# Seven half-width block products in place of eight for two of four batches in a fused mLSTM and gated-cosine kernel

## The chip, the cores and the metric

The kernel runs on one core of a Trainium2 chip. The metric is the device time of one execution in microseconds (us). Beside the times there is one profiled execution. In its listings PE is TensorE with its matmuls, PEld the weight loads of TensorE, DVE is VectorE, ACT is ScalarE, POOL is GpSimd, and SP is the engine whose queue issues most DMA transfers (SPq).

## What is computed

An mLSTM cell with 8 heads of 40 runs over 4 batches of 768 steps. Its output, 3072 rows of 320, goes through a layer with a gated cosine. All data are float32. The scan over time is cut here to its last lines.

```python
def _attn_ref(q, k, v, i_gate, f_gate, o_gate):
    B, H, S, D = q.shape            # 4, 8, 768, 40
    for t in range(S):
        ...
        o = 1.0 / (1.0 + np.exp(-o_gate[:, :, t]))
        y[:, :, t] = o * h_tilde / denom

def _moe_ref(x, w_in, w_out):       # x: 3072 x 320, w_in: 320 x 2048, w_out: 2048 x 320
    h = x @ w_in
    g = h * np.cos(h)
    return g @ w_out
```

The change concerns the last product, g @ w_out, alone.

## The kernel before, in words

The time axis is cut into NC = 6 chunks of C = 128 steps. A chunk c of batch b is cell n = 4c + b. The layer for chunk c needs the cells of that chunk of all four batches, so the layer works one chunk behind: `both_parts(c, b)` computes cell (c+1)*4 + b and a quarter of the layer for chunk c. `first_cells` does the four cells of chunk 0 ahead of the loop. In chunk 5 of the layer no cell is left.

The layer. The 2048 inner columns are 16 blocks of 128, taken two at a time: f2 runs from 0 to 7, and `both_parts` handles f2 = 2b in its first half and 2b + 1 in its second. `Up(c, f2)` multiplies (L613, L616) into two PSUM banks `pup`, one for each of the two blocks e, with the 512 columns being 128 steps of each of four batches. ACT rounds (`near`, L621), DVE takes the remainder (`rest`, L624), ACT takes the sine (`sin`, L629), and DVE multiplies (`gate`, L633) into a tile `g` of 128 x 512, kept as `gs[c, f]`. `down(c, f2)` (L645) then multiplies, for each of the two blocks and each batch, the 128 x 128 part of `g` (the stationary operand, loaded as weights) with the 128 x 320 rows of `w_out_sb`, and accumulates over all 16 blocks in one PSUM tile `po[c][b]` for each batch. So a call is 8 matmuls of 320 columns. On the last call of a chunk (f2 = 7) the matmuls are ordered by batch, and each batch is copied by ACT to `o_sb` (L648, two buffers) and sent out by SP (L649).

Order. The whole order is written out by hand (`tc.manual_schedule()`), and each engine runs its instructions in that order. `down` is called half an iteration after its gates: in the first half of `both_parts`, `down(c, f2 - 1)`, or for b = 0 the last call of the chunk before, `down(c - 1, 7)`; in the second half `down(c, f2)`. On ACT, the first half stands in this order: `near` twice, `sin` twice, then `decay` (L379), the exponential of the next cell's matrix E, and then whatever `down` gives to ACT. The exponential waits for the mask on POOL (`decay_exponents`, L371), and the mask for a subtraction on DVE (L370). After `down`, PE goes on with the cell's values (`values_turned`, L482 and L488), then `Up(c, f2 + 1)`, then the state update (`seam`, L580). DVE's normalisation of the cell (`normalize_turned`, L502 to L514) comes after them, followed by `fade` (L565) and the second half's `rest`.

POOL also scales the keys for the state (`weigh_k`, L392) and, in chunk 0 alone, finishes the weights: the weights come in as float64 bits and are turned into float32 by `parts` (ACT) and `join` (DVE, with the last addition on POOL, L149).

Pools. PSUM has two banks for `ps_a` (the cell), two for `ps_u` (`pup`) and four for `ps_o` (`po`). A wait between engines is set for each tile; a PSUM tile here is a bank or a part of one.

Of the kernel before, what the change touches and what calls it, by code (L numbers as in the profile page):

```python
# [11 lines left out]
FP = mybir.dt.float32  # L12
# [4 lines left out]
OP = mybir.AluOpType  # L17
# [12 lines left out]
def kernel(  # L30
# [20 lines left out]
    nc = tc.nc  # L51

    B, H, S, D = q.shape
    C = 128
    NC = S // C
# [3 lines left out]
    DM = H * D  # L59
    DFF = moe_w_in.shape[1]  # L60
    NF = DFF // 128
# [13 lines left out]
    p2 = ctx.enter_context(tc.tile_pool(name="p2", bufs=2))  # L75
    p3 = ctx.enter_context(tc.tile_pool(name="p3", bufs=3))
    p4 = ctx.enter_context(tc.tile_pool(name="p4", bufs=4))
    pb = ctx.enter_context(tc.tile_pool(name="pb", bufs=5))
    pc = ctx.enter_context(tc.tile_pool(name="pc", bufs=3))
# [3 lines left out]
    ps_o = ctx.enter_context(tc.tile_pool(name="ps_o", bufs=4, space=bass.MemoryType.PSUM))  # L83
# [15 lines left out]
    p1 = ctx.enter_context(tc.tile_pool(name="p1", bufs=1))  # L99
# [20 lines left out]
    w_out_sb = wp.tile([128, NF, DM], FP, name="w_out_sb")  # L120
# [11 lines left out]
    def parts(dst, bits):  # L132
        n = dst.shape[1]
        hi, lo = bits[:, 0:n, 1], bits[:, 0:n, 0].bitcast(U32)
        t = p2.tile([128, WQ], I32, name="wt", tag="wt")[:, 0:n]
        m = p2.tile([128, WQ], I32, name="wm", tag="wm")[:, 0:n]

        nc.scalar.activation(out=t.bitcast(FP), in_=hi.bitcast(FP), func=AF.Abs)

        nc.scalar.activation(out=m, in_=lo, func=AF.Copy, scale=2.0 ** -29)  # L140
        return dst, hi, t, m
# [164 lines left out]
    def sigmoid(c, bs=slice(0, B)):  # L306
        o = sig[c][:, bs.start * DM:bs.stop * DM]
        nc.scalar.activation(out=o, in_=o, func=AF.Sigmoid)
# [51 lines left out]
    def psum_o():  # L360
        return ps_o.tile([128, HP, C], FP, name="pm", tag="o")

    def cols(n, j, width):
        c, b = divmod(n, B)
        return tab[:, c, j, ts(b, H)].unsqueeze(2).to_broadcast([128, H, width])


    def decay_exponents(n):
        E = Es[n]
        nc.vector.tensor_tensor(out=E, in0=E, in1=cols(n, 0, C), op=OP.subtract)  # L370
        nc.gpsimd.affine_select(out=E, in_=E, compare_op=OP.is_ge, fill=1.0e30, base=0,  # L371
                                pattern=[[0, H], [1, C]], channel_multiplier=-1)
# [5 lines left out]
    def decay(n):  # L378
        nc.scalar.activation(out=Es[n], in_=Es[n], func=AF.Exp, scale=-1.0)  # L379
# [9 lines left out]
    def weigh_k(n):  # L389
        if n < N - B:  # L390
            kw = p2.tile([128, H, D], FP, name="kw", tag="kw")
            nc.gpsimd.tensor_tensor(out=kw, in0=ks[n % NB][:, :, 0:D], in1=cols(n, 1, D), op=OP.mult)  # L392
            kws[n] = kw
# [44 lines left out]
    def scores(n):  # L438
        pool, tag = psum(n)
        qT, kT = qkT[n]  # L440
        ps = [pool.tile([128, HP, C], FP, name="ps", tag=tag) for _ in range(2)]
        for p in range(HP):
            for j in range(2):
                r = slice(64 * j, 64 * j + (64 if n < TURNED else D))
                nc.tensor.matmul(ps[j][:, p], kT[r, p], qT[r, p], start=True, stop=True)  # L445
        pss[n] = ps

    def weigh(n):
        for j in range(2):
            w = Es[n].rearrange("p (a j) t -> p a j t", j=2)[:, :, j]  # L450
            nc.vector.tensor_tensor(out=w, in0=pss[n][j], in1=w, op=OP.mult)  # L451

    def values_kept(n):

        pool, tag = (ps_o, "o") if n == B else psum(n)
        heads_of[n] = None
        if n >= B:
            pq = pool.tile([128, H, D1], FP, name="pq", tag=tag)
            for p in range(HP):
                nc.tensor.matmul(pq[:, 2 * p:2 * p + 2].rearrange("p j d -> p (j d)"), qkT[n][0][:, p],  # L460
                                 st[n % B][:, p].rearrange("p j d -> p (j d)"), start=True, stop=True)
            heads_of[n] = pq
# [136 lines left out]
    gs, po = {}, {}  # L599

    class Up:
# [29 lines left out]
        def gate(self, e):  # L631
# [2 lines left out]
                                           op0=OP.mult, op1=OP.mult)  # L634
            gs[self.c, 2 * self.f2 + e] = g

    def down(c, f2):
        if f2 == 0:
            po[c] = [ps_o.tile([128, DM], FP, name="po", tag="o") for _ in range(B)]

        order = [(f, b) for f in (2 * f2, 2 * f2 + 1) for b in range(B)]
        if f2 == NF // 2 - 1:
            order.sort(key=lambda fb: fb[1])
        for f, b in order:
            nc.tensor.matmul(po[c][b], gs[c, f][:, ts(b, C)], w_out_sb[:, f], start=(f == 0), stop=(f == NF - 1))  # L645
            if f == NF - 1:
                o = p2.tile([128, DM], FP, name="o_sb", tag="o_sb")
                nc.scalar.copy(out=o, in_=po[c][b])  # L648
                nc.sync.dma_start(out=out[b * S + c * C:b * S + (c + 1) * C], in_=o)  # L649


    pw, pmu = (ps_u.tile([128, HP, C], FP, name=name, tag="up") for name in ("pw", "pmu"))
# [1 line left out]
    def warm(k, bank=None):  # L654

        for _ in range(k):
            nc.tensor.matmul(bank or pw, nil, nil.unsqueeze(1).to_broadcast([128, HP, 128]), start=True, stop=True)  # L657
# [122 lines left out]
    def out_parts():  # L780
        p, piece = outs.pop(0)
        return p, parts(*piece)

    def out_join(p, h, last=None):
        join(*h, last)
        if p + 3 < NF // 2:
            outs.append((p + 3, weights_out(p + 3)))

    def both_parts(c, b):

        n = (c + 1) * B + b
        cell = n < N
        begin = c == b == 0
        more = cell and n + 1 < N
        f2 = 2 * b
        up = Up(c, f2)
        if cell:  # L800
            scores(n)
            if begin:
                values_kept(n)

                warm(6, psum_o())
        for e in range(2):
            up.near(e)
        if begin:
            weigh(n)
        for e in range(2):  # L810
            up.rest(e)
        if cell and not begin:
            weigh(n)
        if begin or more and c > 0:
            decay_exponents(n + 1)
        for e in range(2):
            up.sin(e)
            up.gate(e)
        if c == 0 and b == 1:
            sigmoid(1, slice(1, B))  # L820
        if b == B - 1 and c + 2 < NC:
            sigmoid(c + 2)
        h = ()
        if begin:
            h = out_parts()
            w = parts(*pieces.pop(0))
        else:
            if c == 0:
                out_join(*out_parts())
            if pieces:  # L830
                join(*parts(*pieces.pop(0)))
        if begin or more and c > 0:
            decay(n + 1)
        elif more:
            decay_by_bias(n + 1)
        if f2 > 0:
            down(c, f2 - 1)
        elif c > 0:
            down(c - 1, NF // 2 - 1)
        if cell:  # L840
            if n + 2 < N:
                load(n + 2)
            if n < TURNED:
                if not begin:
                    values_kept(n)
                values(n)
                normalize(n)
            else:
                values_turned(n)
            if begin:  # L850
                out_join(*h, nc.vector)
            if TURNED <= n + 2 < N:
                load_G(n + 2)
            if n + 3 < N:
                load_E(n + 3)
            if b == B - 2 and c + 2 < NC:
                load_o(c + 2)
            if n >= TURNED:
                normalize_turned(n)
            fade(n)  # L860
        h = w if begin else ()
        if not begin:
            sin_next()
        if pieces and not begin:
            h = parts(*pieces.pop(0))
        up = Up(c, f2 + 1)
        if cell:
            seam(n)
        for e in range(2):
            up.near(e)  # L870
        for e in range(2):
            up.rest(e)
        if cell and n < TURNED:
            seam_out(n)
        if h:
            join(*h)
        if cell:
            state(n)
        for e in range(2):
            up.sin(e)  # L880
            up.gate(e)
        if more:
            weigh_k(n + 1)
        if pieces:
            join(*parts(*pieces.pop(0)))
        down(c, f2)
        if pieces:
            join(*parts(*pieces.pop(0)))
        if c == 0:
            if b + 2 < B:  # L890
                pieces.extend(weights_in(b + 2))
            h = out_parts()
        if more and n + 1 < TURNED:
            turn(n + 1)
            turn_out(n + 1, c > 0)
        elif more:
            turn_blocks(n + 1)
        if c == 0:
            out_join(*h)
# [38 lines left out]
```

## Time and profile before

| | us |
|---|---|
| median of 4 runs | 551.47 |
| range of the runs | 550.1 to 551.79 |
| the profiled execution's own time | 550.1 |
| its span, first to last instruction | 548.4 |

The profiled execution's mean granted TensorE clock was 0.997. The groups that bear on the change, from the list of groups by line (us busy in total, mean ns of one):

| line, engine, what | count | busy us | mean ns |
|---|---|---|---|
| L645 PE, down | 768 | 219.3 | 439 |
| L613 PE, up | 384 | 175.0 | 598 |
| L645 PEld, its weight loads | 768 | 142.0 | 190 |
| L371 POOL, mask of E | 19 | 20.7 | 1091 |
| L392 POOL, keys scaled | 20 | 14.4 | 722 |
| L648 ACT, output copied from PSUM | 24 | | 425 (median) |
| L649 SPq, output issued | 24 | | 349 (median) |

How to read it: durations of matmuls and loads overlap those of their neighbours, so the busy time of a group is less than count times mean, and what a matmul costs in a stream is seen from the distance of starts. A timeline line gives start, length, engine, line, operation, tiles and, in brackets, idle time before it and what ended it. The float32 matmul is carried out as two passes, each with its weight load, so counts are twice those of the program.

### The profile page before, as it was taken

To read this page: it belongs to the slowest core of one execution; us is meant where nothing else is said; L and a number is where in the kernel's file an instruction comes from. 1 tells how busy PE (TensorE), PEld (TensorE's weight loads), DVE (VectorE), ACT (ScalarE), POOL (GpSimd) and SP (SyncE) were. 2 spreads that over 40 slices of the span, in tenths; PEclk is the share of its full clock that TensorE was granted. 3 is DMA by queue.
4 is the path that set the end of the run, shared out by engine and by line. 5 is a ranking of instruction groups with operands and counts; after the bars stand their busy time and mean duration, and the time that the engine had idled before them with its cause. 6 is when DMAs were issued, how large, how long until landed. Compare 5 with 4: busy or idle time off the path is not lost.

```text
span 548.4 us, 9153 instructions
## 1 busy us (share of the span) xinstructions
PE 538.0 (98%) x3395; PEld 316.7 (58%) x3395; DVE 355.7 (65%) x692; ACT 264.4 (48%) x420; POOL 76.5 (14%) x112
## 2 busy tenths in 40 slices
PE   9989899999999999999999999999999999999997
PEld 6865566665565565565565555555555655555554
DVE  5877987967767677677677667667666666232311
ACT  4868796775632543633445344427335423231312
POOL 5531433523110110100101101100000000000000
PEclk9989999999999999999999999999999999999999
DMA  9999995961366761166735076635075000100001
GB/s 146 208 229 222 236 226 136 194 125 28 87 138 126 148 129 30 58 131 135 152 83 99 26 158 135 141 79 117 3 175 110 7 14 12 53 0 1 0 0 49
DMA packets 134509, 56.82 MB, mean 104 GB/s; under 512 B 72081, under 2 KB 130529, under 8 KB 134465
## 3 DMA queue, kind: packets, MB, share of 16 engines
q1 hardware_dynamic: 134320, 56.04, 47.3%
q8 instruction: 27, 0.44, 0.4%
q0 software_dynamic: 96, 0.18, 0.2%
q14 instruction: 18, 0.14, 0.1%
q10 hardware_dynamic: 48, 0.02, 0.0%
HBM read 50.00 MB, written 6.21 MB: 103 GB/s over the span
## 4 chain that ended last, share of the span: by engine, by line
PE 89%; DVE 4%; DMA 3%; ACT 1%; issue 1%; SPq 0%; POOL 0%; ACTq 0%; DVEq 0%; POOLq 0%
PE po L645 37%; PE pup L613 29%; PE pup L616 9%; PE ps L445 4%; PE hp L488 3%; PE hp L482 2%; PE ph L470 2%; PE pu L580 1%; PE pw L657 1%; DMA o<-in_o_gate_dram 1%; DMA ks<-in_k_dram 1%; PE pt L426 1%; DMA bits<-in_moe_w_out_dram 1%; PE px L573 1%; DVE wt L148 1%
## 5 line engine op out<-in xcount | busy, mean ns | idle before, releaser
L645 PE MATMUL po<-w_out_sb,g 128*128 128x320 f32 x768 | 219.3, 439 | 1.3 <-POOL w_out_sb L149 1.0
L645 PEld LDWEIGHTS po<-w_out_sb,g 128*128 128x128 f32 x768 | 142.0, 190 | 67.0 <-issue 8.3
L613 PE MATMUL pup<-xT,w_in_sb 128*128 128x512 f32 x384 | 175.0, 598 | 1.1 <-POOL w_in_sb L149 0.6
L621 ACT ACTIVATE n<-pup 128x512 int32<-128x512 f32 x96 | 52.0, 593 | 213.2 <-PE pup L616 213.2
L624 DVE SCALAR_TENSOR_TENSOR n<-pup,n 128x512 f32<-128x512 f32 x96 | 61.8, 686 | 135.1 <-ACT n L621 135.1
L613 PEld LDWEIGHTS pup<-xT,w_in_sb 128*128 128x128 f32 x384 | 70.9, 190 | 77.5 <-issue 64.2
L629 ACT ACTIVATE n<-n 128x512 f32<-128x512 f32 x96 | 58.8, 630 | 11.9 <-DVE n L624 11.9
L633 DVE SCALAR_TENSOR_TENSOR g<-pup,n 128x512 f32<-128x512 f32 x96 | 61.7, 684 | 1.7
L371 POOL TENSOR_SCALAR_AFFINE_SELECT E<-E 128x1024 f32<-128x1024 f32 x19 | 20.7, 1091 | 291.1 <-DVE E L370 268.1
L616 PE MATMUL pup<-xT,w_in_l 64*128 64x512 f32 x192 | 54.2, 641 | 0.0
L616 PEld LDWEIGHTS pup<-xT,w_in_l 64*128 64x128 f32 x192 | 14.4, 184 | 36.4 <-issue 35.6
L451 DVE TENSOR_TENSOR E<-ps,E 128x512 f32<-128x512 f32 x48 | 30.7, 680 | 4.7 <-PE ps L445 4.7
L379 ACT ACTIVATE E<-E 128x1024 f32<-128x1024 f32 x21 | 22.2, 1057 | 22.3 <-POOL E L371 16.3
L410 DVE STREAM_TRANSPOSE t<-qs 128x512 f32<-128x512 f32 x32 | 32.3, 1086 | 0.0
L445 PEld LDWEIGHTS ps<-t,t 40*128 40x128 f32 (+1 forms) x384 | 25.1, 188 | 9.7 <-issue 9.2
L445 PE MATMUL ps<-t,t 40*128 40x128 f32 (+1 forms) x384 | 25.8, 274 | 0.0
L379 ACT ACT_TABLE_LOAD x18 | 23.1, 1283 | 0.3
L778 ACT ACT_TABLE_LOAD x18 | 23.1, 1283 | 0.3
L502 DVE STREAM_TRANSPOSE room<-hp 128x128 f32<-128x128 f32 x32 | 8.6, 306 | 22.5 <-PE hp L488 22.5
L370 DVE TENSOR_TENSOR E<-E,tab 128x1024 f32<-128x1024 f32 x19 | 23.1, 1215 | 0.0
L488 PE MATMUL hp<-E,vs 128*32 128x128 f32 x512 | 17.3, 276 | 0.0
L417 DVE STREAM_TRANSPOSE room<-o 128x256 f32<-128x256 f32 x32 | 17.2, 617 | 0.0
(128 smaller groups left out, 427.9 us busy)
## 6 DMA issues: line engine op xcount, KB each, us to landing
E<-M_d SPq DMA_DIRECT2D x22, 512.0 KB
bits<-in_moe_w_in_dram SPq DMA_DIRECT2D x40, 128.0 KB
bits<-in_moe_w_out_dram SPq DMA_DIRECT2D x8, 640.0 KB
room<-G_d SPq DMA_DIRECT2D x32, 128.0 KB
ks<-in_k_dram SPq DMA_DIRECT2D x24, 160.0 KB
vs<-in_v_dram SPq DMA_DIRECT2D x24, 160.0 KB
out_dram<-o_sb SPq DMA_DIRECT2D x24, 160.0 KB
qs<-in_q_dram SPq DMA_DIRECT2D x32, 80.0 KB
```

The lines of the kernel that those rows point to most:

```text
L379: nc.scalar.activation(out=Es[n], in_=Es[n], func=AF.Exp, scale=-1.0)
L410: nc.vector.transpose(out=dst.rearrange("r p (t x) -> r p x t", x=T4), in_=src.rearrange("r p (x d) -> r p x d", x=T4)[:, :, :, 0:32])
L445: nc.tensor.matmul(ps[j][:, p], kT[r, p], qT[r, p], start=True, stop=True)
L451: nc.vector.tensor_tensor(out=w, in0=pss[n][j], in1=w, op=OP.mult)
L488: nc.tensor.matmul(hps[n][j][ts(p, 32), half], vs[n % NB][:, h, lo:lo + DA], Es[n][:, h], start=False, stop=True, skip_group_check=True)
L613: nc.tensor.matmul(pu, w_in_sb[:, i, ts(block(f2, e), 128)], x(i), start=(i == 0), stop=False)
L616: nc.tensor.matmul(pu, w_in_l[r, f2], x(NK, r), start=False, stop=True)
L621: nc.scalar.activation(out=self.n[e], in_=self.pu[e], func=AF.Copy, bias=0.25)
L624: nc.vector.scalar_tensor_tensor(out=self.n[e].bitcast(FP), in0=self.pu[e], scalar=0.25, in1=self.n[e], op0=OP.add, op1=OP.subtract)
L629: nc.scalar.activation(out=r, in_=r, func=AF.Sin, scale=TWO_PI_DOWN)
L633: nc.vector.scalar_tensor_tensor(out=g, in0=self.pu[e], scalar=TWO_PI, in1=self.n[e].bitcast(FP), op0=OP.mult, op1=OP.mult)
L645: nc.tensor.matmul(po[c][b], gs[c, f][:, ts(b, C)], w_out_sb[:, f], start=(f == 0), stop=(f == NF - 1))
```

## The change

For chunks 1 to 5 (`parted(c)`), the products of batches 0 and 1 with a pair of blocks are formed as a 2 x 2 block product with seven multiplications in place of eight (the scheme of Strassen in Winograd's form). The left factor has four 128 x 128 parts: batch 0 or 1, block 0 or 1. The right factor has four 128 x 160 parts: block 0 or 1, left or right half of the columns. Batches 2 and 3 are multiplied as before (`whole`).

- `differences` (POOL): four 128 x 160 combinations of the w_out parts for each pair p, once, kept in `T`; done two pairs at a time (`two_differences`), at the end of chunk 0 and in chunk 1.
- `sums` (POOL): four 128 x 128 combinations of the g parts for each call, in `sg`, placed after the gates.
- `down_parted` (PE): 4 matmuls of 320 columns, then 7 of 160 columns. The seven products accumulate over all eight pairs: six stand in banks 0 and 1, three each; the seventh region, `Ps[6]`, stands in bank 2 beside batch 2's 320 columns.
- At the last pair of a chunk, batches 2 and 3 are copied by ACT and sent as before. `Ps[0]` is copied by ACT, and seven additions on DVE combine the products into the outputs of batches 0 and 1, which are then sent. In the very last call of the program the seven products come first, and batches 3 and 2 after them.

```diff
+    def differences(p, T):
+        B11, B12, B21, B22 = (w_out_sb[:, 2 * p + e, ts(h, DH)] for e in range(2) for h in range(2))
+        for i, (x, y) in enumerate(((B12, B11), (B22, T[:, 0]), (B22, B12), (T[:, 1], B21))):
+            nc.gpsimd.tensor_tensor(out=T[:, i], in0=x, in1=y, op=OP.subtract)
+        Ts[p] = T
...
+    def sums(c, f2):
...
+        S = p2.tile([128, 4, C], FP, name="sg", tag="wt")
+        A11, A21, A12, A22 = (gs[c, 2 * f2 + e][:, ts(b, C)] for e in range(2) for b in range(2))
+        for i, (x, y, op) in enumerate(((A21, A22, OP.add), (S[:, 0], A11, OP.subtract),
+                                        (A11, A21, OP.subtract), (A12, S[:, 1], OP.subtract))):
+            nc.gpsimd.tensor_tensor(out=S[:, i], in0=x, in1=y, op=op)
...
+    def down_parted(c, f2):
+        end = f2 == NF // 2 - 1
...
+            po[c] = [ps_o.tile([128, 3 * DH + 32], FP, name="po", tag="o") for _ in range(4)]
+        banks = po[c]
+        Ps = [banks[i // 3][:, ts(i % 3, DH)] for i in range(6)] + [banks[2][:, DM:DM + DH]]
...
+        def whole(bs=range(2, B)):
+            for b in bs:
+                for e, (g, w) in enumerate(((g0, w0), (g1, w1))):
+                    product(banks[b][:, 0:DM], g[:, ts(b, C)], w, e == 0)
+                if end:
+                    o = p2.tile([128, DM], FP, name="o_sb", tag="o_sb")
+                    nc.scalar.copy(out=o, in_=banks[b][:, 0:DM])
+                    result(c, b, o)
+        very_end = end and c == NC - 1
+        if not very_end:
+            whole()
+        product(Ps[0], g0[:, 0:C], w0[:, lo], True)
+        product(Ps[1], g1[:, 0:C], w1[:, lo], False)
+        product(Ps[3], g1[:, C:2 * C], T[:, 3], True)
+        product(Ps[4], S[:, 0], T[:, 0], False)
+        product(Ps[5], S[:, 1], T[:, 1], False)
+        product(Ps[6], S[:, 2], T[:, 2], False)
+        product(Ps[2], S[:, 3], w1[:, hi], False)
+        if end:
...
+            nc.scalar.copy(out=U[:, 0], in_=Ps[0])
+            for dst, x, y, op in ((o0[:, lo], U[:, 0], Ps[1], OP.add), (U[:, 0], U[:, 0], Ps[5], OP.add),
+                                  (U[:, 1], U[:, 0], Ps[6], OP.add), (U[:, 0], U[:, 0], Ps[4], OP.add),
+                                  (o0[:, hi], U[:, 0], Ps[2], OP.add), (o1[:, lo], U[:, 1], Ps[3], OP.subtract),
+                                  (o1[:, hi], U[:, 1], Ps[4], OP.add)):
+                nc.vector.tensor_tensor(out=dst, in0=x, in1=y, op=op)
+            if very_end:
+                whole((3, 2))
+            for b, o in enumerate((o0, o1)):
+                result(c, b, o)
...
     def down(c, f2):
+        if parted(c):
+            down_parted(c, f2)
+            return
...
         for e in range(2):
             up.sin(e)
             up.gate(e)
+        sums(c, f2)
...
         for e in range(2):
             up.sin(e)
             up.gate(e)
+        sums(c, f2 + 1)
         if more:
             weigh_k(n + 1)
+        if c == 0 and b == B - 1 or c == 1 and b < B - 1:
+            two_differences(c * (2 * b + 2))
```

More of the change, by code (lines that the diff above doesn't have):

```diff
@@ L635, in gate, with parted, two_differences @@
             gs[self.c, 2 * self.f2 + e] = g
+    DH = DM // 2
+    Ts, sg = {}, {}
+    def parted(c):
+        return c > 0
+    def differences(p, T):
[3 more added lines that the diff above has]
+        Ts[p] = T
+    def two_differences(p):
+        if p < 6:
+            T = pc.tile([128, 2, 4, DH], FP, name="T", tag="bits")
+            for e in range(2):
+                differences(p + e, T[:, e])
+        else:
+            for e in range(2):
+                differences(p + e, pb.tile([128, 4, DH], FP, name="T", tag="bits"))
@@ new lines, in sums @@
+    def sums(c, f2):
+        if not parted(c):
+            return
[4 more added lines that the diff above has]
+            nc.gpsimd.tensor_tensor(out=S[:, i], in0=x, in1=y, op=op)
+        sg[c, f2] = S
@@ new lines, in down_parted, with product @@
+    def down_parted(c, f2):
+        end = f2 == NF // 2 - 1
+        if f2 == 0:
+            po[c] = [ps_o.tile([128, 3 * DH + 32], FP, name="po", tag="o") for _ in range(4)]
+        banks = po[c]
+        Ps = [banks[i // 3][:, ts(i % 3, DH)] for i in range(6)] + [banks[2][:, DM:DM + DH]]
+        g0, g1 = (gs[c, 2 * f2 + e] for e in range(2))
+        w0, w1 = (w_out_sb[:, 2 * f2 + e] for e in range(2))
+        S, T = sg[c, f2], Ts[f2]
+        lo, hi = slice(0, DH), slice(DH, DM)
+        def product(out, g, w, first):
+            nc.tensor.matmul(out, g, w, start=(f2 == 0 and first), stop=end, skip_group_check=True)
+        def whole(bs=range(2, B)):
[17 more added lines that the diff above has]
+        if end:
+            o2 = p2.tile([128, 2, DM], FP, name="o2", tag="wm")
+            o0, o1 = (o2[:, b] for b in range(2))
+            U = p1.tile([128, 2, DH], FP, name="hs", tag="hs")
+            nc.scalar.copy(out=U[:, 0], in_=Ps[0])
[8 more added lines that the diff above has]
+                result(c, b, o)
@@ L637, in down, with result @@
+    def result(c, b, o):
+        nc.sync.dma_start(out=out[b * S + c * C:b * S + (c + 1) * C], in_=o)
     def down(c, f2):
+        if parted(c):
+            down_parted(c, f2)
+            return
         if f2 == 0:
@@ L648, in down @@
                 nc.scalar.copy(out=o, in_=po[c][b])
-                nc.sync.dma_start(out=out[b * S + c * C:b * S + (c + 1) * C], in_=o)
+                result(c, b, o)
     pw, pmu = (ps_u.tile([128, HP, C], FP, name=name, tag="up") for name in ("pw", "pmu"))
```

## The prediction

> **What bounds the kernel now.** I read the page's busy shares first, then the chain of work that ended last.
>
> ```profile
> PE 538.0 (98%) x3395; PEld 316.7 (58%) x3395; DVE 355.7 (65%) x692; ACT 264.4 (48%) x420; POOL 76.5 (14%) x112
> ...
> PE 89%; DVE 4%; DMA 3%; ACT 1%; issue 1%; SPq 0%; POOL 0%; ACTq 0%; DVEq 0%; POOLq 0%
> ```
>
> TensorE (PE) is busy nearly throughout, and 89% of the chain is matmuls. So each ns that a matmul pass saves shortens the kernel, each ns that PE idles lengthens it, and work on POOL or DVE is free until PE waits for it. The list of groups by shape shows what a pass is:
>
> ```profile
> L645 PE MATMUL po<-w_out_sb,g 128*128 128x320 f32 x768 | 219.3, 439 | 1.3 <-POOL w_out_sb L149 1.0 <-DVE w_out_sb L149 0.3
> ...
> L470 PE MATMUL ph<-vs,E 128*128 128x41 f32 x128 | 15.5, 282 | 0.2 <-DVE E L451 0.2
> ```
>
> A float32 matmul is two passes: 6 chunks x 16 blocks x 4 batches is 384, and the row has 768. A pass's own duration (439 ns) holds its latency; what counts is the distance from one start to the next. The timeline of the weight loads gives it:
>
> ```profile
> 8.93 0.97 PEld L357 LDWEIGHTS pm<-M_rows,ident 128*128 128x128 f32 x8
> ...
> 30.78 1.86 PEld L470 LDWEIGHTS ph<-vs,E 128*128 128x128 f32 x16
> ...
> 301.44 0.19 PEld L613 LDWEIGHTS pup<-xT,w_in_sb 128*128 128x128 f32 x1 [0.24 <-issue]
> 301.87 0.19 PEld L613 LDWEIGHTS pup<-xT,w_in_sb 128*128 128x128 f32 x1 [0.24 <-issue]
> ```
>
> 512 columns: 0.43 us apart, 0.84 ns a column. 41 columns would stream in 0.034, yet sixteen loads take 1.86: (1.86-0.19)/15 = 0.111. 128 columns: (0.97-0.19)/7 = 0.111. So a pass costs the larger of 0.111 (its weight load) and 0.84 ns a column.
>
> **The sum on PE.** The change acts on chunks 1 to 5, 8 pairs each: 40 calls. A call was 16 passes of 320 columns, 0.269 each: 4.30 us. (The timeline's 16 loads last 4.07 = 0.11 for the first, exposed load + 14 x 0.269 + 0.19.) Now 8 such passes stay (2.15), and 7 products x 2 passes have 160 columns: 0.134 by the column, and I take 0.136 for a small fixed part: 1.90. Gain 0.248 a call, x 40 = **9.9 us**. Only beyond 2.15/14 = 0.154 would there be none.
>
> A rule speaks against this: the Trainium skill, "TensorE: Matmul & The Clock Gate", section "The mechanism", says that a weight load overlaps a running matmul only when the row groups differ. Here every load fills all 128 rows. By that rule a narrow pass would be 0.107+0.134 = 0.241, so 14 of them 3.37, a loss of 1.2 us a call, 49 in all. But by it the 320-column pass would be 0.376, and it is 0.269; L357's 0.111 also excludes it. The rows decide.
>
> **What is hidden.** POOL gets four 128x128 sums a call, after the second gate. Nearest row: 128x320 (L392) 722 ns; so about 0.4 each, 1.7 a call, some 65 us in all, on an engine 86% idle. They are needed half an iteration later (gates end 310.77, the next down begins at 317.30): slack over 5 us. The exponentials' mask (L371) stands ahead of them; weigh_k behind them is wanted only in the next iteration. The weight differences, 32 of 128x160 at about 0.45, come in four bursts of 3.6 us behind weigh_k; in chunk 0 that is from 127.2 to 131, before the last w_out join (135.44). A DVE operation with two SBUF inputs may wait for a POOL one: the z product beside L386 took 1.17 us against 0.39 mean, but the gates read PSUM and took 681 ns either way. They finish about 1 us or more before PE wants their banks. Cost 0; without this cover, up to 1.7 a call. The added waits of PE on POOL, if already satisfied, cost nothing: loads with such waits also start 0.111 apart.
>
> **Where the cover is missing.** At a chunk's last pair, PE finishes batch 2 in bank 2, ACT copies it out, and the sixth product goes into the same bank. In the built program's order, exactly these products carry a wait on ACT besides POOL. That copy stands on ACT behind the exponential of the next cell. The timeline of such an end (chunk 2's):
>
> ```profile
> 306.06 4.58 PE L645 MATMUL po<-w_out_sb,g 128*128 128x320 f32 x16
> ...
> 308.36 1.21 DVE L370 TENSOR_TENSOR E<-E,tab 128x1024 f32<-128x1024 f32 x1
> ...
> 309.71 1.09 POOL L371 TENSOR_SCALAR_AFFINE_SELECT E<-E 128x1024 f32<-128x1024 f32 x1 [19.34 <-DVE E L370]
> ...
> 310.83 1.06 ACT L379 ACTIVATE E<-E 128x1024 f32<-128x1024 f32 x1 [1.62 <-POOL E L371]
> ...
> 311.80 0.73 ACT L648 COPY o_sb<-po 128x320 f32<-128x320 f32 x2
> ```
>
> Mask, exponential and copy come one after the other, and the first copy (425 ns) ends at 312.2. Before, PE had no need of it. Now the sixth product is due at 306.06 + 0.10 + 8x0.269 + 10x0.136 = 309.67. It must wait until 312.2, plus 0.06 to wake and 0.107 for a load with no matmul over it: **2.7 us**. Behind it in PE's queue stand the seventh product, the cell's values and the next Up: all is late. The ends of chunks 1 and 3 have the same distances (down 221.55, copy 227.29; 390.57 and 396.31): 3 x 2.7 = **8.1 us**. Bounds: 0 if the wait is for something earlier, 8.5 as computed with slower waking. Chunk 4 ends beside no cell: copy from about 475.2 to 475.6, product due at 476.06: free.
>
> **The clock.** 2.7 us without a matmul may cost more. Windows of 3.4 us on the clock's own grid, with their granted clock (the number before the DMA share):
>
> ```profile
> 30.50:33.90 3.40, 2.89 (x36) 2.51 (x33) 3.01 (x5) 3.11 (x10) 1.27 (x1) 1.00 1.15 121
> 33.90:37.30 3.40, 2.79 (x11) 1.78 (x10) 3.23 (x10) 0.41 (x2) 1.26 (x1) 0.50 1.00 253
> 37.30:40.70 3.40, 3.18 (x24) 1.64 (x23) 1.69 (x3) 2.48 (x6) 1.50 (x2) 1.00 1.11 345
> ```
>
> The same skill page, section "What's actually happening", has the clock fall to half after a whole idle window of about 3.4 us; by it 2.7 us costs nothing. But the window at 30.5 had no gap over 0.6 us, and the next ran at half clock. It held mostly 41-column passes; from columns x 0.84 ns its array streamed 39% of the time. Windows at 53% and more (95 us, for one) kept the clock. A window that holds most of the 2.7 us streams 20 to 40%. With the limit between 39 and 53%, it must hold 1.6 to 2.0 us of the stall, which a random phase does in 6 to 9 of 10. Each half window loses 1.7 us of matmuls. I take two of three: **3.4 us** (0 to 5.1).
>
> **Chunk ends on DVE, and the tail.** Seven additions of 128x160 (L596, 40x164 with PSUM, has 318 ns: about 0.32 each, chained) and a short copy are 2.6 us after the seventh product, at four places inside. They delay the turned normalisation; by the timeline it is done at 315.8 and DVE's next work came at 318.1. With the stall both move: DVE would be ready near 319.4, as PE's Up ends (319.2) and its first result reaches DVE at 319.9; the hp banks are free by 318, PE wants them at 319.2. Just covered. Four PSUM copies fall to two, which also ends ACT's wait for output transfers (2.76 us, off the path). At the very end batch 2's matmuls share bank 2 with the sixth product and wait for the third addition: about 1.5 after the seventh product against 1.08 of batch 3, so 0.5 with its load. Then SP issues batch 2 and behind it batches 0 and 1 (median 349 ns each): 0.7 more, and three 160 KB transfers close together, up to 0.8. Tail **+1.5 us** (1.0 to 2.3).
>
> **Sum** against the profiled run (span 548.4, own time 550.1): -9.9 + 8.1 + 3.4 + 1.5 = +3.1, so 553.2. The four runs' median is 551.47, 1.4 above that run; the forecast for a median is **554.6 us**. About 0.2% (1.1 us) is what a measurement of this kernel can tell from no change.
>
> **The rivals.**
> - No clock loss: the stalls stand, the page's rule holds or the phases miss. -0.3: 551.2, no change. For it: the rule. Against it: the 39% window. Chance 0.2, with the case of a single half window.
> - No stall: the sixth product doesn't wait for the copy, or ACT gets to it earlier. -9.9+1.5: about **543**, faster. For it: every other part of the change is covered. Against it: the order on ACT and the wait on that product. It decides when the copy ends before 309.7. Chance 0.14.
> - Exposed loads: narrow passes above 0.154, up to 0.241, 600 us. L357 and L470 exclude it; 0.02.
> - The forecast, the stalls with two or three half windows: 0.64, its own range 552.6 to 557.
>
> The range is 550.4 to 557.5: it takes in the first rival and leaves out the second and third. Chances: faster 0.15, same 0.2, slower 0.65.
>
> **What would show it.** The row of 160-column passes x560 with starts 0.136 apart (0.154 would break the gain). In the waits, PE for the output copy, 3 times, about 2.6 us each; if absent, the second rival. Slices with a granted clock of 7 or 8 tenths near 225, 309 and 393; if absent, the first. POOL's busy time near 155 us, with no wait of PE on it.

## The result and the profile after

| | before | after |
|---|---|---|
| median us | 551.26 (55 runs) | 552.81 (34 runs) |
| lowest to highest | 549.04 to 552.13 | 549.35 to 558.72 |
| ratio, 95% interval | | 1.0035 [1.0023, 1.0048] |
| profiled execution: own time, span | 550.1, 548.4 | 554.27, 552.4 |
| its mean granted TensorE clock | 0.997 | 0.986 |

By the ratio of the means the kernel became 0.35% slower, by 1.9 us; the medians differ by 1.55. Two of the runs after, at 558.1 and 558.7 us, count as slow and are left out of the ratio. The forecast was 3.1 us slower, 0.56%. First the page of the kernel after: busy shares, the clock row and the chain that ended last.

```profile
PE 532.3 (96%) x3635; PEld 337.0 (61%) x3635; DVE 369.0 (67%) x727; ACT 261.7 (47%) x415; POOL 168.0 (30%) x304
...
PEclk9799999999999999899999899999999999999999
...
PE 82%; DVE 9%; ACT 3%; POOL 2%; issue 1%; SPq 1%; DMA 1%; POOLq 0%; DVEq 0%; ACTq 0%
```

PE is busy for 96% of a longer span, where it was 98%: it has begun to wait. (Its share of the chain, 82% for 89%, is no proof of that: it is 82% and 83% in the two cures below too, where PE is busy for 98%.) The clock row has an 8 in slices 17 and 23, at about 225 and 310 us, where it had only nines before; the 7 in slice 2 belongs to the first cells. In the new kernel's lines L689 is a matmul of `down_parted`, L672 a sum on POOL, L697 the copy of a whole batch, L714 the small copy of `Ps[0]` and L719 the additions. For the wait, the list of groups by shape:

```profile
L689 PE MATMUL po<-w_out_sb,g 128*128 128x320 f32 x320 | 97.0, 445 | 0.4 <-DVE hs L719 0.4
...
L689 PE MATMUL po<-T,sg 128*128 128x160 f32 x240 | 40.0, 301 | 7.5 <-POOL sg L672 7.5
```

Nearly all new idle time of PE in the layer, 7.5 us, stands before products with a sum from POOL (0.4 more is in the tail). The row names POOL as what ended it. The timeline of the end of chunk 2 shows that this name is wrong:

```profile
302.32 0.46 POOL L672 TENSOR_TENSOR sg<-g 128x128 f32<-128x128 f32 x1 [7.99 <-DVE g L633]
...
303.69 0.46 POOL L672 TENSOR_TENSOR sg<-g,sg 128x128 f32<-128x128 f32 x1
...
311.34 0.71 PE L689 MATMUL po<-T,sg 128*128 128x160 f32 x4
...
313.04 1.06 ACT L379 ACTIVATE E<-E 128x1024 f32<-128x1024 f32 x1 [1.62 <-POOL E L371]
...
314.00 0.73 ACT L697 COPY o_sb<-po 128x320 f32<-128x320 f32 x2
...
314.55 0.66 PE L689 MATMUL po<-T,sg 128*128 128x160 f32 x2 [2.51 <-POOL sg L672]
```

The sums for this pair were done at 304.15, seven microseconds before PE came to them. (POOL was by then at the next chunk's sums, and one of those ended near 314.5.) What ended just before PE went on is the first of the two ACT copies, 314.00 + 0.41; it stands behind the exponential. In all three stalls the load of the waiting product starts 0.11 us after that copy's end. A sum of the next chunk ends within 0.01 us of it in all three as well, for the exponential and these sums both follow the mask; the second experiment below tells the two apart. The product waited for both engines, and the profile put the wait down to the wrong one.

The clock, in windows along the clock's own grid (PEclk is the granted clock), at chunk 1's end and at this one. A window at half clock is called a half window below.

```profile
core 0: us, PE busy (x) PEld busy (x) DVE busy (x) ACT busy (x) POOL busy (x), PEclk, DMA share, GB/s
...
226.00:229.40 3.40, 1.73 (x52) 1.39 (x56) 0.64 (x3) 2.59 (x5) 1.85 (x5) 1.00 0.27 95
229.40:232.80 3.40, 3.40 (x28) 1.83 (x20) 3.16 (x14) 0.88 (x2) 0.00 (x0) 0.51 0.32 103
...
311.40:314.80 3.40, 0.89 (x7) 0.68 (x6) 1.58 (x3) 1.71 (x4) 2.69 (x5) 1.00 0.00 0
314.80:318.20 3.40, 3.40 (x65) 2.57 (x67) 1.96 (x7) 1.78 (x3) 0.13 (x1) 0.50 0.27 96
```

After each of these stalls PE is busy for a whole window, at half its clock.

The sum of the two profiled executions, by stretches of the timeline from the first Up matmul of one chunk to that of the next; the clock column is half the length of the half-clock windows in the stretch that delay matmuls:

| stretch | before | after | difference | of it clock | new calls | stall |
|---|---|---|---|---|---|---|
| first cells | 38.14 | 39.71 | +1.57 | +1.71 | 0 | |
| layer chunk 0 | 93.40 | 93.40 | 0 | 0 | 0 | |
| chunk 1 | 84.53 | 82.79 | -1.74 | 0 | 7 | |
| chunk 2 | 84.51 | 86.89 | +2.38 | +1.71 | 8 | yes |
| chunk 3 | 84.51 | 86.79 | +2.28 | +1.71 | 8 | yes |
| chunk 4 | 82.77 | 83.50 | +0.73 | 0 | 8 | yes |
| chunk 5 and end | 80.49 | 79.32 | -1.17 | 0 | 9 | |

A chunk's last call falls into the next stretch, so chunk 1 has seven new calls and no stall: -1.74 / 7 = -0.25 a call. The calls themselves say the same: from a call's first matmul to the Up matmul behind it 4.159 us, where it was 4.411, so 0.252 less. Chunk 4 has a stall without a lost window: +0.73 + 8 x 0.252 = 2.7. The first cells are untouched by the change. All the kernels here share them, and their profiles have one or two half windows there; in this pair it was two after and one before.

### The profile page after: what moved, and what is told of

The parts are those of the page before. It is cut to its first block, busy times and chain, and to the rows that moved or that the text cites. A ratio compares the mean times of both kernels' runs of the same rounds, so it can differ in the third digit from the quotient of the medians.

```text
span 552.4 us, 9941 instructions
## 1 busy us (share of the span) xinstructions
PE 532.3 (96%) x3635; PEld 337.0 (61%) x3635; DVE 369.0 (67%) x727; ACT 261.7 (47%) x415; POOL 168.0 (30%) x304
## 4 chain that ended last, share of the span: by engine, by line
PE 82%; DVE 9%; ACT 3%; POOL 2%; issue 1%; SPq 1%; DMA 1%; POOLq 0%; DVEq 0%; ACTq 0%
PE po L689 29%; PE pup L613 29%; PE pup L616 9%; PE po L739 4%; PE hp L488 3%; PE ps L445 3%; PE hp L482 2%; DVE n L624 1%; PE pu L580 1%; DVE wt L146 1%; PE ph L470 1%; DVE wt L148 1%; DVE E L370 1%; DMA o<-in_o_gate_dram 1%; DVE E L451 1%
## 5 line engine op out<-in xcount | busy, mean ns | idle before, releaser
L689 PE MATMUL po<-w_out_sb,g 128*128 128x320 f32 (+1 forms) x480 | 118.9, 397 | 0.4 <-DVE hs L719 0.4
L689 PEld LDWEIGHTS po<-w_out_sb,g 128*128 128x128 f32 x480 | 83.5, 190 | 37.4 <-issue 9.1
L672 POOL TENSOR_TENSOR sg<-g 128x128 f32<-128x128 f32 x80 | 36.5, 457 | 204.2 <-DVE g L633 202.7
L689 PE MATMUL po<-T,sg 128*128 128x160 f32 x240 | 40.0, 301 | 7.5 <-POOL sg L672 7.5
L689 PEld LDWEIGHTS po<-T,sg 128*128 128x128 f32 x240 | 34.8, 190 | 8.2 <-POOL sg L672 8.2
L739 PE MATMUL po<-w_out_sb,g 128*128 128x320 f32 x128 | 36.6, 439 | 1.3 <-POOL w_out_sb L149 1.0
L739 PEld LDWEIGHTS po<-w_out_sb,g 128*128 128x128 f32 x128 | 23.7, 190 | 11.0 <-POOL w_out_sb L149 1.3
```

Source lines behind the costliest of these rows:

```text
L672: nc.gpsimd.tensor_tensor(out=S[:, i], in0=x, in1=y, op=op)
L689: nc.tensor.matmul(out, g, w, start=(f2 == 0 and first), stop=end, skip_group_check=True)
```

## The experiments

My theory was that of the prediction: three stalls on the late copy, and half-clock windows as their consequence. The rivals: the sums on POOL (which the profile itself names), and a clock that falls because the passes are narrow.

**The sixth product ahead of batch 2.** At the ends of chunks 1 to 4 the product that shares bank 2 is issued before batch 2, so no copy comes between.

```diff
+        if end and not very_end:
+            product(Ps[6], S[:, 2], T[:, 2], False)
         if not very_end:
             whole()
...
-        product(Ps[6], S[:, 2], T[:, 2], False)
+        if not end or very_end:
+            product(Ps[6], S[:, 2], T[:, 2], False)
```

> At the ends of chunks 1 to 4 the sixth product is issued before batch 2, so it no longer shares its bank with a copy that is still to come. My theory (three stalls of 2.67 us on the copy of batch 2, each able to cost a clock window): the waits go, the granted clock returns to that of before, and the time is before - 40 x 0.254 + 1.1 of tail = about 542.3 us, ratio 0.984. Rival A (the wait is for the sums on POOL, as the list of waits names it): unchanged, near 552.8. Rival B (the half windows come from the narrow passes, not from the stalls): the stalls go but the clock stays near 0.989, about 545.

Measured: 542.52 us, ratio 0.9846 [0.9833, 0.986]. The stall is gone: stretches 2 and 3 took 82.84 and 82.85 where 86.89 and 86.79 had been. No half window is left after the first cells, and the profiled clock is 0.993. Both rivals fall: the sums on POOL are unchanged and nobody waits for them, and the narrow passes are all there. One small wait was new:

```profile
226.71 0.31 ACT L717 COPY hs<-po 128x160 f32<-128x160 f32 x1
227.05 0.32 DVE L722 TENSOR_TENSOR o<-hs,po 128x160 f32<-128x160 f32 x1 [1.99 <-ACT hs L717]
...
230.72 0.71 DVE L511 TENSOR_TENSOR room<-room,hp 128x256 f32<-128x256 f32 x2
...
231.24 0.51 PE L580 MATMUL pu<-vs,kw 128*40 128x41 f32 x16 [0.27 <-DVE room L511]
```

The small copy still stands behind the exponential, so the seven additions and with them the normalisation come late, and PE's seam waits 0.3 us for its bank. With the stall gone this is the next in line.

**The copies ahead of the exponential.** The bank stays shared; ACT does the copies first.

```diff
+        late = b == 0 and c > 1
-        if begin or more and c > 0:
+        if begin or more and c > 0 and not late:
             decay(n + 1)
-        elif more:
+        elif more and not late:
             decay_by_bias(n + 1)
...
             down(c - 1, NF // 2 - 1)
+        if late and more:
+            decay(n + 1)
```

> The sixth product and the copy stay in one bank, but at the first cell of chunks 2 to 5 ACT does the copies before the next cell's exponential. Theory (the copy is late only because it stands behind the exponential, 312.2 where 309.7 was needed): the copy ends near 308.4, no stall, 542 to 543, as in the first experiment; the exponential moves by about 0.3 us and nobody waits for it. If the shared bank itself or the sums were the cause: unchanged, 552.8.

Measured: 541.21 us, ratio 0.9823 [0.9809, 0.9836], the fastest of all. Its timeline at the end of chunk 2:

```profile
302.69 2.96 PE L689 MATMUL po<-w_out_sb,g 128*128 128x320 f32 x12
...
304.44 0.41 ACT L697 COPY o_sb<-po 128x320 f32<-128x320 f32 x1
...
305.76 0.98 PE L689 MATMUL po<-T,sg 128*128 128x160 f32 x6
...
307.04 0.29 ACT L714 COPY hs<-po 128x160 f32<-128x160 f32 x1 [1.48 <-PE po L689]
307.36 1.28 ACT L379 ACT_TABLE_LOAD   x1
...
308.65 1.06 ACT L379 ACTIVATE E<-E 128x1024 f32<-128x1024 f32 x1
```

The copy is done at 304.85, before the sixth product is due, and the six passes, the sixth product's among them, run without a break. The next chunk's sums on POOL, one of which ended just as PE went on in the stalls, begin only at 307.54 here, after these passes, so PE doesn't wait for those either. The small copy is early too, so the seam waits for nobody: stretches 2 and 3 take 82.50, which is 84.51 - 8 x 0.252 = 82.49. The exponential ends 7.02 us after the down began (309.71 against 302.69), 1.2 us later than the 5.83 of before (311.89 against 306.06), not the 0.3 that I had put down: its table load (1.28 us) now stands behind the copies too. Nobody waited for it.

**The stalls filled.** Before the sixth product PE runs matmuls of zeros into a free bank, as long as the stall lasts or for a part of it. Nothing reads that bank's zeros.

```diff
+        if end and c < NC - 2:
+            warm(11, ps_a.tile([128, HP, C], FP, name="fill", tag="a"))
         product(Ps[6], S[:, 2], T[:, 2], False)
```

> The stalls stay, but PE runs eleven bf16 matmuls of zeros (0.215 us each, 2.4 us) in each of the three, before the sixth product. Theory (idle time in a window halves the next one): the time between instructions stays as it is, the half windows at 229 and 315 us are gone, and the median falls by the 3.4 us that I charged to the clock, to about 549.5, with a spread as narrow as before. Rival (the skill page's whole idle window is needed, and the half windows have another cause): unchanged, 552.8 with its wide spread.

> As the run with eleven matmuls of zeros, but five (1.1 us): each stall keeps its length, and 1.4 us of it stay idle. Theory (a window of 3.4 us must hold 1.6 to 2.0 us of idle time to halve the next): no half window after 100 us, the same time as with eleven, about 549.8. Rival (any gap of over a microsecond counts): half windows in some runs, time between 549.8 and 552.8.

> Two matmuls of zeros: 2.1 us of each stall stay idle, in one piece, at the limit that I estimated. Theory: a phase must put nearly the whole gap in one window, which 4 to 6 of 10 do, so half windows come back, fewer than without the filling: median 551 to 552.5, spread of several us. Rival (a gap must be nearly a whole window of 3.4 us, or the half windows had another cause): as with eleven, 549.8.

| matmuls of zeros | idle in a stall, about | median us | lowest to highest | ratio to before | median of the runs' granted clock |
|---|---|---|---|---|---|
| 0 (the change as it is) | 2.5 | 552.81 | 549.35 to 558.72 | 1.0035 | 0.989 |
| 2 | 2.1 | 550.99 | 548.54 to 552.06 | 0.9994 | 0.992 |
| 5 | 1.4 | 548.48 | 548.05 to 550.91 | 0.997 | 0.998 |
| 11 | 0.1 | 549.76 | 547.82 to 551.08 | 0.9987 | 0.995 |

The profile with eleven, at the end of chunk 1:

```profile
223.53 2.54 PE L753 MATMUL fill<-nil 128*128 128x512 bf16 x11
...
225.65 0.73 ACT L697 COPY o_sb<-po 128x320 f32<-128x320 f32 x2
226.20 0.51 PE L689 MATMUL po<-T,sg 128*128 128x160 f32 x2
```

The sixth product still waits for the copy, so each stall costs its 2.7 us as before (stretches 2 and 3 take 85.25 against 82.50 without a stall), and yet the median is 3.1 us lower, or 2.6 by the ratios to the runs of the kernel before that stand beside each: that part was the clock, and it was the idle time that brought it. With five the profile has no half window in the layer either. Five lies below eleven, but their ratios to before, 0.997 [0.9955, 0.9985] and 0.9987 [0.9973, 1.0], overlap; runs also differ by one or two half windows of 1.7 us in the first cells, which these kernels share with the one before. With two, the result lies just below what I had put down (551 to 552.5). Its one profile has no half window at the stalls, but its runs' clocks (0.986 to 0.999) are on the whole lower than with five (0.990 to 0.999), so some probably had them. The ratios' intervals with two, [0.9979, 1.001], and with five overlap slightly, so this step is not shown. How many of its windows belong to the stalls and how many to the first cells, the clocks of the runs don't tell.

**POOL's sums twice.** On top of the first experiment.

```diff
         sg[c, f2] = S
+        R2 = p1.tile([128, 2, C], FP, name="sg2", tag="sg2")
+        for i, (x, y, op) in enumerate(((A21, A22, OP.add), (R2[:, 0], A11, OP.subtract),
+                                        (A11, A21, OP.subtract), (A12, R2[:, 1], OP.subtract))):
+            nc.gpsimd.tensor_tensor(out=R2[:, i % 2], in0=x, in1=y, op=op)
```

> On top of the first experiment each group of four sums on POOL is followed by a second, unused one: POOL busy from 168 to about 205 us. Theory (POOL's work is hidden): the same time as the first experiment within 0.5 us. Rival (POOL's sums hold up DVE[...], or come late for the products): slower by 1 us or more, up to 1.7 a call where the cover is gone.

Measured: 542.39 us against 542.52 without the second set. POOL was busy for 242.0 us, not 205: there are 160 more sums, 0.46 to 0.54 us each by their rows, 80 us in all, where I had counted 37; the scaling of the keys (L392) took 6 us less. Even so doubling them costs nothing that can be seen: stretches 2 and 3 take 82.85 each, against 82.84 and 82.85. They are hidden, with about as much room again.

## Why the prediction held, point by point

- *The gain on PE*, 40 x 0.248 = 9.9 us: it was 0.25 a call in the chunk without a stall. Narrow passes start 0.136 apart, as put down. The four merged passes at 311.34 show it: 0.71 us for three distances and a last pass of 0.30, as this shape's row has it. The overlap rule of the Trainium skill ("TensorE: Matmul & The Clock Gate", section "The mechanism"), which asked for 0.241, does not hold here.
- *The stalls*, 3 x 2.7 = 8.1 us: three, at the three places, and none at the end of chunk 4. The profile has 2.5 us of idle time for each, and with the exposed load 2.7. The cause is shown by two independent cures: taking the product out of the copy's way, or taking the exponential out of the copy's.
- *The clock*, two half windows of three, 3.4 us: the profile has exactly two, which in a single profile is chance. The third stall (398.8 to 401.3) straddles an edge of the grid at about 400.1, so that each window holds under 1.3 us of it. Over the runs the loss is span x (1 - clock): at the medians 6.1 us after and 3.3 before (38 runs beside the experiments), so 2.8 more. That counts half windows at the very end too, where no matmul is left (1.0 us of the profile's). It goes with the spread of the runs over 9 us: the slowest have clocks of 0.978 and 0.980, the fastest 0.995. The estimate stood on a misread share: the window at 30.5 us streams 39% only if matmuls that overlap are counted twice, and 34% otherwise. What the runs show of the limit stands at the end.
- *The tail*, +1.5 us (1.0 to 2.3): the last stretch changed by -1.17, and nine calls should give -2.27; so 1.1. The wait of batch 2's matmuls for the third addition is there, 0.37 us and a load:

```profile
546.55 1.34 PE L689 MATMUL po<-w_out_sb,g 128*128 128x320 f32 x4 [0.37 <-DVE hs L719]
```

- *Hidden work*: right. POOL's busy time was 168.0 where I had said 155, without consequence: the sums took 0.457 us each and not 0.4, the differences 0.52 and not 0.45, and the scaling of the keys, which I had left as it was, 1.03 and not 0.72. The additions' 2.6 us on DVE stayed covered beside the stalls, and as soon as the stalls were gone 0.3 us of them was not (the first experiment): the cover that I called "just" was no more than that.
- *What I would have misread*: I had written that a wait of PE on POOL would speak against me. The list does name POOL, 7.5 us. Only the dates of the sums, and then the experiments, tell that it wasn't.

The sum with the measured terms: -40 x 0.252 + 3 x 2.75 + 1.1 + 2.8 = +2.1, against a measured +1.9. The stall is a whole call's time with it and without, 7.00 - 4.25. The terms behind the rest of the forecast of +3.1 are the clock (2.8 for 3.4), the tail (1.1 for 1.5) and a gain of 10.1 for 9.9. Against the forecast of the median, 554.6, the measured 552.81 is 1.8 lower: 1.2 by these terms, 0.2 by the kernel before (551.26 for 551.47), and 0.4 because the medians lie closer together than the means. The rival without stalls, 543, is what the two cures measured: 542.5 and 541.2.

## What to carry to other kernels

When an edit puts a second tenant into a PSUM bank, look up who reads the first one and what stands before that reader on its engine: here ten microseconds of gain hung on a copy behind an exponential, and moving either gave nearly all of it. A stall on PE of a few microseconds can cost more than its length, by the clock in the window after it. And where an instruction waits for two engines, check the dates of both before believing the name that the profile gives.

## What the runs showed of the hardware

The clock judges a window by how much of it the array streams, rather than by the length of a gap. I worked that share out from the matmul starts and columns x 0.84 ns (overlaps counted once), in the windows of the clock's grid, for the kernel before, the changed one and the six experiments. Eleven half-clock stretches, of one or two windows, begin inside the work: ten came after windows that streamed 19 to 39%, one after 44% (chunk 1's stall, 1.6 us idle in its window). Four windows at full clock with 40 to 45% were not followed by one, and none of those with 46% or more. So the share decides but for a narrow band, and the length of the idle time does not: a window with 1.9 us idle (at 35.2 us, with two fills) kept the clock at 40%, and one with 0.4 us idle (at 18.7 us, with eleven) lost it at 39%. A gap of 2.5 us is therefore enough or not, depending on where the grid cuts it, and the grid lies differently in each run. The Trainium skill, "TensorE: Matmul & The Clock Gate", section "What's actually happening", states a whole idle window of about 3.4 us; much less was enough here. Matmuls of zeros count as activity: with five or eleven of them in a stall the profiles have no half window there, and the medians of the runs' clocks are 0.998 and 0.995 in place of 0.989.

Loads of all 128 rows overlapped running matmuls throughout, down to passes of 0.136 us, and waits on POOL that were already satisfied added nothing to that: six such passes take 0.98 us above, five distances of 0.136 and a last pass of 0.30.
